# Attention heads into a two-layer network: earlier input loads on other queues, and a later place for the softmax reciprocals

## The chip, the core and the metric

The kernel runs on one core of a Trainium2 chip. The core has five instruction streams: TensorE (PE, matrix products), VectorE (DVE), ScalarE (ACT), GpSimd (POOL) and SyncE (SP). Each works through its own list in order; semaphores tie the lists together. DMA transfers can be issued from SP, ACT and POOL. The metric is the device time in microseconds (us), as the median of several runs.

## What is computed

The reference takes q, k and v of shape (8 images, 12 heads, 448 positions, 64) and two weight matrices, 768 x 2048 and 2048 x 768. All are float32. Cut to what matters:

```python
scores = scale * q @ k.T                 # per image and head, scale = 1/sqrt(64)
attn   = exp(scores - max)               # softmax over the last axis
attn   = attn / (attn.sum(-1) + 1e-9)
x      = attn @ v                        # heads side by side: 3584 tokens x 768
h      = x @ w_in                        # 3584 x 2048
out    = maximum(0.01 * h, h) @ w_out    # 3584 x 768
```

## The kernel before, in words

**Work units.** Two heads of one image make a pair, so an image has 6 pairs and the whole input has 48. The 448 positions are cut into 4 chunks of 112. The order of all instructions is written out by hand; no planner moves them.

**One pair.** `load` brings q, k and v of the pair in as float32, three transfers of 224 KB. `cast` turns them into bfloat16; the v tiles carry a block of ones beside v, so that the product with v also yields the row sums of the exponentials. `transposes` turns q and k on PE and DVE copies the result to SBUF (qkT). `scores` makes one chunk of k against all q for both heads, and `expo` takes the exponential on ACT. `pv` multiplies the exponentials of one head (j = 0 or 1) with v; DVE copies the result to a tile t, and SP sends the row of sums from t to a tile in which the sums lie across partitions (sums). `recips` waits for that, takes the reciprocal on DVE (rec), and SP writes it to DRAM (d) and reads it back twice, broadcast over 64 partitions each (rb). `muls` multiplies t with rb on DVE and writes the slice of xT that belongs to this pair. xT is the input of the network, with tokens along the free axis.

**The network.** `mlp(i)` works on a block of 384 or 512 tokens (`cuts`), alternating, as 448 is no multiple of 128. It makes 16 tiles of h, each from 6 products over xT (line 233), with the leaky ReLU on ACT, and then the output in rows of 128 tokens, each half from 16 products (line 245) with a copy on DVE (line 250) and a store on SP. It is a generator that yields after each product, so it can be spread between other work.

**The order.** A pair step u has eight slots, s0 to s7. In step u the scores of pair u are made (s0 and s4, exponentials in s0, s1, s4, s5), the products with v of pair u-1 (s2 and s6), and the transposes of pair u+1 (s7). Before the change `recips(u-2)` stands in s1 and `muls(u-2)` in s7. POOL loads pair u+6 and, in the first steps, two weight transfers in s0, and casts pair u+2 in s3. The first 8 steps run without the network: that is the head. From then on the products of one block are spread evenly over the 48 slots of six steps, beginning with slot s0. Each block starts just after the last `muls` it needs. The last block runs alone at the end.

**Start.** Before the first step, the identity for the transposes is made on POOL, the ones in the v tiles are set on DVE, and POOL issues the loads of pairs 0 to 5 with the casts of pairs 0 and 1 between them. The weights are cast from float32 to bfloat16 by the transfer itself, in eight pieces of 768 KB (as written), on POOL.

Lines of the profile to know: 94 loads, 106, 107 and 109 casts, 129 weights, 148 and 152 transposes and their copy, 160 scores, 170 exponentials, 176 products with v, 181 their copy to t, 186 sums, 190 reciprocal, 192 d, 195 rb, 208 multiply into xT, 224 stores.

Of the kernel before, what the change touches and what calls it, by code (L numbers as in the profile page):

```python
# [10 lines left out]
BF16 = mybir.dt.bfloat16  # L11
# [6 lines left out]
def kernel(  # L18
# [9 lines left out]
    nc = tc.nc  # L28

    B, H, S, D = q.shape  # L30
    DM, DF = moe_w_in.shape
    P = 128
    HP = H // 2
    SC = 112
    NSC = S // SC
    KD = DM // P
    MD = DF // P
    NW = DM // 2
    NU = B * HP
    scale = 1.0 / float(D) ** 0.5  # L40

    cuts = [((b * S) // P) * P for b in range(B)] + [B * S]
# [3 lines left out]
    const_pool = ctx.enter_context(tc.tile_pool(name="const", bufs=1))  # L46
    w_pool = ctx.enter_context(tc.tile_pool(name="weights", bufs=1))
    ld_pool = ctx.enter_context(tc.tile_pool(name="ld", bufs=6))
    cast_pool = ctx.enter_context(tc.tile_pool(name="cast", bufs=3))
    v_pool = ctx.enter_context(tc.tile_pool(name="vones", bufs=1))  # L50
    qk_pool = ctx.enter_context(tc.tile_pool(name="qk", bufs=3))
    exp_pool = ctx.enter_context(tc.tile_pool(name="exp", bufs=3))
    t_pool = ctx.enter_context(tc.tile_pool(name="pvt", bufs=3))
    r_pool = ctx.enter_context(tc.tile_pool(name="rec", bufs=3))
    xT_pool = ctx.enter_context(tc.tile_pool(name="xT", bufs=3))
    h_pool = ctx.enter_context(tc.tile_pool(name="h", bufs=2))
# [5 lines left out]
    ps_pv = ctx.enter_context(tc.tile_pool(name="ps_pv", bufs=1, space=PSUM))  # L62
    ps_mm = ctx.enter_context(tc.tile_pool(name="ps_mm", bufs=2, space=PSUM))

    ident = const_pool.tile([P, P], BF16)
    make_identity(nc, ident)

    NV = 4  # L70
    v_sb = [v_pool.tile([SC, 2, NSC, 2 * D], BF16, name=f"v{i}") for i in range(NV)]
    for t in v_sb:
        nc.vector.memset(t[:, 0, :, D:], 1.0)
        nc.vector.memset(t[:, 1, :, :D], 1.0)

    w_in_sb = w_pool.tile([P, KD, DF], BF16)
    w_out_sb = w_pool.tile([P, MD, DM], BF16)
# [4 lines left out]
    q_sb = {}  # L82
    k_sb = {}

    def load(u):
        if u >= NU:
            return
        b, hp = divmod(u, HP)  # L90
        raw[u] = []
        for a, name in ((q, "fq"), (k, "fk"), (v, "fv")):
            t = ld_pool.tile([SC, 2, NSC, D], F32, name=name)
            nc.gpsimd.dma_start(  # L94
                out=t.rearrange("p h so d -> p h (so d)"),
                in_=a[b, 2 * hp:2 * hp + 2].rearrange("h (p so) d -> p h (so d)", so=NSC),
            )
            raw[u].append(t)

    def cast(u):  # L100
        if u >= NU:
            return
        fq, fk, fv = raw.pop(u)
        q_sb[u] = cast_pool.tile([SC, NSC, 2, D], BF16, name="q")
        k_sb[u] = cast_pool.tile([SC, NSC, 2, D], BF16, name="k")
        nc.gpsimd.tensor_copy(q_sb[u].rearrange("p so h d -> p h so d"), fq)  # L106
        nc.gpsimd.tensor_copy(k_sb[u].rearrange("p so h d -> p h so d"), fk)  # L107
        for j in range(2):
            nc.gpsimd.tensor_copy(v_sb[u % NV][:, j, :, j * D:(j + 1) * D], fv[:, j])  # L109

    load(0)
    cast(0)
    load(1)
    load(2)
    load(3)
    cast(1)
    for i in range(4, 6):
        load(i)
    w_steps = []
    for i in range(4):  # L120
        w_steps.append((w_in_sb[:, :, ts(i, DF // 4)], w_in_v[:, :, ts(i, DF // 4)]))
# [3 lines left out]
    def load_w(n):  # L125
        for _ in range(n):
            if w_steps:
                o, i = w_steps.pop(0)
                nc.gpsimd.dma_start(out=o, in_=i)


    qk_t = {}
# [5 lines left out]
    def get_xT(i):  # L138
        if xT[i] is None:
            xT[i] = xT_pool.tile([P, KD, 4 * P], BF16, name="xT")  # L140
        return xT[i]

    def transposes(u):
        b, hp = divmod(u, HP)
        tr = ps_tr.tile([P, 2, S], BF16, name="tr")
        for i, src in enumerate((q_sb[u], k_sb[u])):
            for so in range(NSC):
                nc.tensor.transpose(  # L148
                    tr[:, i, ts(so, SC)], src[:, so], ident[:SC, :SC]
                )  # L150
        qk_t[u] = qk_pool.tile([P, 2, S], BF16, name="qkT")
        nc.vector.tensor_copy(qk_t[u], tr)  # L152
# [14 lines left out]
    def expo(u, c):  # L167
        if u not in e_t:
            e_t[u] = exp_pool.tile([SC, 2, NSC, S], BF16, name="e")
        nc.scalar.activation(e_t[u][:, :, c, :], sc_t.pop((u, c))[:, :, :S], AX.Exp, scale=scale)  # L170

    def pv(u, j):
        b, hp = divmod(u, HP)
        ps = ps_pv.tile([P, S], F32, name="pv")
        for c in range(NSC):
            nc.tensor.matmul(  # L176
                ps, v_sb[u % NV][:, j, c, :], e_t[u][:, j, c, :],
                start=(c == 0), stop=(c == NSC - 1),
# [9 lines left out]
    def recips(u):  # L188
        rec = r_pool.tile([SC, 2, NSC], F32, name="rec")
        nc.vector.reciprocal(rec, bc_t[u])  # L190
        d = d_pool.tile([2, S], F32, name="d")
        nc.sync.dma_start(out=d.rearrange("j (p c) -> p j c", c=NSC), in_=rec)
        rb = r_pool.tile([P, S], F32, name="rb")
        for j in range(2):
            nc.sync.dma_start(out=rb[ts(j, D), :], in_=d[j:j + 1, :].to_broadcast([D, S]))  # L195
        bc_t[u] = rb

    def muls(u):
        b, hp = divmod(u, HP)
        lo, hi = b * S, (b + 1) * S  # L200
        for j in range(2):
            pl = slice(j * D, (j + 1) * D)
            for i in (b, b + 1):
                a, z = max(lo, cuts[i]), min(hi, cuts[i + 1] if i < B else hi)
                if a >= z:
                    continue
                x = get_xT(i)
                nc.vector.tensor_mul(  # L208
                    x[pl, hp, a - cuts[i]:z - cuts[i]],
                    pv_s[u, j][pl, a - lo:z - lo],  # L210
                    bc_t[u][pl, a - lo:z - lo],
                )
        del pv_s[u, 0], pv_s[u, 1], bc_t[u], e_t[u], qk_t[u]
# [13 lines left out]
    def mlp(i):  # L227
        n = cuts[i + 1] - cuts[i]
        h = h_pool.tile([P, MD, 4 * P], BF16, name="h")
        for m in range(MD):  # L230
            ps = ps_mm.tile([P, 4 * P], F32, name="mm")
            for kk in range(KD):
                nc.tensor.matmul(  # L233
                    ps[:, :n], w_in_sb[:, kk, ts(m, P)], get_xT(i)[:, kk, :n],
                    start=(kk == 0), stop=(kk == KD - 1),
                )
                if kk == KD - 1:
                    nc.scalar.activation(h[:, m, :n], ps[:, :n], AX.Prelu, alpha=0.01)  # L238
                yield n
        for c in range(n // P):  # L240
            o = o_pool.tile([P, DM], F32, name="o")
            for w in range(2):
                ps = ps_mm.tile([P, 4 * P], F32, name="mm")
                for m in range(MD):
                    nc.tensor.matmul(  # L245
                        ps[:, :NW], h[:, m, ts(c, P)], w_out_sb[:, m, ts(w, NW)],
                        start=(m == 0), stop=(m == MD - 1),
                    )
                    if m == MD - 1:
                        nc.vector.tensor_copy(o[:, ts(w, NW)], ps[:, :NW])  # L250
                    yield NW
            store(o, cuts[i] + c * P)


    def slots(u):

        on = u < NU

        def s0():
            if on:  # L260
                scores(u, 0)
                scores(u, 1)
                expo(u, 0)
            load(u + 6)
            if u < 6:
                load_w(2)

        def s1():
            if on:
                expo(u, 1)  # L270
            if u >= 2:
                recips(u - 2)

        def s2():
            if 1 <= u <= NU:
                pv(u - 1, 0)

        def s3():
            cast(u + 2)

        def s4():
            if on:
                scores(u, 2)
                scores(u, 3)
                expo(u, 2)

        def s5():
            if on:
                expo(u, 3)

        def s6():
            if 1 <= u <= NU:
                pv(u - 1, 1)

        def s7():
            if u + 1 < NU:
                transposes(u + 1)
            if u >= 2:
                muls(u - 2)

        return [s0, s1, s2, s3, s4, s5, s6, s7]

    transposes(0)
    for i in range(B + 1):

        first = 0 if i == 0 else HP * i + 2
        last = HP * (i + 1) + 2 if i < B else first
        work = [s for u in range(first, min(last, NU + 2)) for s in slots(u)]
        atoms = mlp(i - 1) if i > 0 else iter(())
        total = 0 if i == 0 else MD * KD * (cuts[i] - cuts[i - 1]) + (cuts[i] - cuts[i - 1]) // P * MD * DM  # L310
        used = 0
        for n, s in enumerate(work):
            s()
            while used < total * (n + 1) // len(work):
                step = next(atoms, None)
                if step is None:
                    break
                used += step
        for _ in atoms:
            pass  # L320
# [30 lines left out]
```

## Time and profile before

| | us |
|---|---|
| three runs | 555.23, 542.29, 554.82 |
| median of the runs | 554.82 |
| the profiled execution, its own time | 556.75 |
| span of that execution, first to last instruction | 555.0 |
| head, until the network's first products | 0 to 97 |
| seven blocks beside the pair steps | 97 to 507 |
| last block alone | 507 to 555 |

Busy time in these three parts, each line with its length, then busy time (and number of instructions) of PE, PEld (the loading of stationary operands, beside PE), DVE, ACT and POOL, the granted TensorE clock, the mean share of the DMA engines and GB/s:

```profile
0.00:97.00 97.00, 48.50 (x201) 18.92 (x202) 27.08 (x59) 30.36 (x35) 59.90 (x107) 0.77 0.86 189
97.00:507.00 410.00, 386.95 (x2400) 196.87 (x2399) 183.68 (x334) 191.34 (x271) 142.18 (x244) 0.98 0.39 102
507.00:555.00 48.00, 43.09 (x218) 21.85 (x217) 4.46 (x8) 9.56 (x16) 0.00 (x0) 0.93 0.15 42
```

How to read what follows. A group of instructions is named by its line, engine and operation and by the tiles it writes and reads ("xT<-t,rb"). "[4.59 <-DMA rb<-d]" behind an instruction says that its engine stood idle for 4.59 us before it and that the landing of that transfer ended the wait. The chain of waits is followed back from the last instruction, at each step to what released it; its shares say where the span was spent.

### The profile page before, as it was taken

What the parts mean: (1) busy time and instruction counts of PE and PEld (TensorE: products, weight loads), DVE (VectorE), ACT (ScalarE), POOL (GpSimd) and SP (SyncE); (2) the same over time, 40 slices, a digit from 0 to 9 for tenths busy, and PEclk for the clock granted to TensorE, in tenths of its full rate; (3) what the DMA queues carried; (4) which work ended last, traced back from release to release, by engine and by line L of the source; (5) the groups of instructions that cost most, each with busy time, mean ns of one, the idle gap of its engine ahead of it and who ended that gap; (6) DMA issues with size and microseconds to landing.
All of it is one profiled execution on the core that took longest, in us unless ns stands there. A gap on an engine that the chain in (4) does not pass through costs nothing.

```text
span 555.0 us, 7636 instructions
## 1 busy us (share of the span) xinstructions
PE 478.5 (86%) x2816; PEld 237.6 (43%) x2816; DVE 215.2 (39%) x400; ACT 231.3 (42%) x321; POOL 202.1 (36%) x350
## 2 busy tenths in 40 slices
PE   2744447999899999999599999999699999996996
PEld 1211113455444554555244554555244555552453
DVE  2221335444433564444234545464253553341011
ACT  3332223563346334654165335644365246601400
POOL 8963724454532433643225335455141210000000
PEclk9998555999989999999799999999899999997999
DMA  5999944344533354535433436354341222122013
GB/s 147 249 230 242 242 109 103 98 118 120 156 96 83 89 155 123 135 90 154 113 82 94 122 102 172 97 145 115 95 118 30 79 62 50 31 63 60 1 28 87
DMA packets 52774, 62.21 MB, mean 112 GB/s; under 512 B 28672, under 2 KB 39936, under 8 KB 52736
## 3 DMA queue, kind: packets, MB, share of 16 engines
q0 software_dynamic: 16768, 39.33, 27.8%
q1 hardware_dynamic: 35968, 22.38, 16.6%
q8 instruction: 22, 0.36, 0.3%
q14 instruction: 16, 0.13, 0.1%
HBM read 56.62 MB, written 11.18 MB: 122 GB/s over the span
## 4 chain that ended last, share of the span: by engine, by line
PE 65%; DMA 22%; DVE 7%; SPq 2%; issue 2%; POOL 2%; DVEq 0%; POOLq 0%
PE mm L233 25%; PE mm L245 19%; PE pv L176 11%; DMA d<-rec 8%; DMA sums<-t 7%; DMA rb<-d 7%; PE sc L160 6%; DVE xT L208 3%; PE tr L148 3%; DVE qkT L152 2%; SPq L195 1%; DVE o L250 1%; DMA fv<-in_v_dram 1%; SPq L224 1%; POOL fq L94 0%
## 5 line engine op out<-in xcount | busy, mean ns | idle before, releaser
L170 ACT ACTIVATE e<-sc 112x896 bf16<-112x896 f32 x192 | 168.5, 915 | 188.8 <-PE sc L160 188.6
L233 PE MATMUL mm<-xT,w_in_sb 128*128 128x384 bf16 (+1 forms) x768 | 173.0, 364 | 20.9 <-DVE xT L208 19.4
L245 PE MATMUL mm<-w_out_sb,h 128*128 128x384 bf16 x896 | 162.1, 326 | 0.8 <-DVE o L250 0.6
L176 PE MATMUL pv<-e,v 112*128 112x448 bf16 x384 | 100.9, 390 | 29.9 <-DVE t L181 29.9
L109 POOL CAST v<-fv 112x256 bf16<-112x256 f32 x96 | 38.3, 404 | 230.9 <-PE pv L176 230.6
L181 DVE COPY t<-pv 128x448 f32<-128x448 f32 x96 | 59.6, 620 | 149.0 <-PE pv L176 148.7
L233 PEld LDWEIGHTS <-w_in_sb 128*128 128x128 bf16 x768 | 72.0, 100 | 102.7 <-issue 47.7
L238 ACT ACTIVATE h<-mm 128x384 bf16<-128x384 f32 (+1 forms) x128 | 69.9, 546 | 109.2 <-PE mm L233 109.1
L208 DVE TENSOR_TENSOR xT<-t,rb 64x384 bf16<-64x384 f32 (+2 forms) x144 | 87.1, 630 | 68.2 <-DMA rb<-d 67.0
L245 PEld LDWEIGHTS <-h 128*128 128x128 bf16 x896 | 83.6, 98 | 67.0 <-issue 13.7
L176 PEld LDWEIGHTS <-v 112*128 112x128 bf16 x384 | 38.9, 103 | 74.7 <-issue 47.8
L160 PE MATMUL sc<-qkT 64*112 64x448 bf16 x384 | 63.4, 411 | 8.6 <-DVE qkT L152 6.4
L250 DVE COPY o<-mm 128x384 f32<-128x384 f32 x56 | 31.1, 555 | 63.6 <-PE mm L245 63.1
L152 DVE COPY qkT<-tr 128x896 bf16<-128x896 bf16 x48 | 30.0, 624 | 33.5 <-PE tr L148 32.8
L160 PEld LDWEIGHTS <-qkT 64*112 64x112 bf16 x384 | 18.7, 135 | 45.6 <-DVE qkT L152 24.8
L94 POOL DMA_DIRECT2D fv<-in_v_dram x48 | 31.9, 664 | 11.9 <-DMA w_in_sb<-in_moe_w_in_dram 6.5
L106 POOL CAST q<-fq 112x512 bf16<-112x512 f32 x48 | 34.0, 708 | 4.2 <-PE tr L148 1.5
L94 POOL DMA_DIRECT2D fk<-in_k_dram x48 | 31.9, 665 | 7.2 <-DMA w_out_sb<-in_moe_w_out_dram 4.6
L94 POOL DMA_DIRECT2D fq<-in_q_dram x48 | 32.1, 668 | 4.6 <-issue 0.2
L107 POOL CAST k<-fk 112x512 bf16<-112x512 f32 x48 | 31.8, 662 | 0.1
L148 PE MATMUL tr<-ident,q 112*128 112x112 bf16 x192 | 19.3, 228 | 11.2 <-POOL q L106 11.2
L148 PEld LDWEIGHTS <-q 112*128 112x128 bf16 x192 | 15.4, 106 | 21.1 <-POOL q L106 12.4
(14 smaller groups left out, 52.8 us busy)
## 6 DMA issues: line engine op xcount, KB each, us to landing
fq<-in_q_dram POOLq DMA_DIRECT2D x48, 224.0 KB, 3.4
fk<-in_k_dram POOLq DMA_DIRECT2D x48, 224.0 KB, 3.9
fv<-in_v_dram POOLq DMA_DIRECT2D x48, 224.0 KB, 4.2
rb<-d SPq DMA_DIRECT2D x96, 112.0 KB, 3.0
w_in_sb<-in_moe_w_in_dram POOLq DMA_DIRECT2D x4, 768.0 KB, 12.7
w_out_sb<-in_moe_w_out_dram POOLq DMA_DIRECT2D x4, 768.0 KB, 17.7
out_dram<-o SPq DMA_DIRECT2D x8, 336.0 KB, 3.3
out_dram<-o SPq DMA_DIRECT2D x8, 288.0 KB, 2.7
```

The lines of the kernel that those rows point to most:

```text
L94: nc.gpsimd.dma_start(out=t.rearrange("p h so d -> p h (so d)"), in_=a[b, 2 * hp:2 * hp + 2].rearrange("h (p so) d -> p h (so d)", so=NSC),)
L109: nc.gpsimd.tensor_copy(v_sb[u % NV][:, j, :, j * D:(j + 1) * D], fv[:, j])
L148: nc.tensor.transpose(tr[:, i, ts(so, SC)], src[:, so], ident[:SC, :SC])
L152: nc.vector.tensor_copy(qk_t[u], tr)
L160: nc.tensor.matmul(ps[:, j, :S], qk_t[u][j * D:(j + 1) * D, 1, ts(c, SC)], qk_t[u][j * D:(j + 1) * D, 0, :], start=True, stop=True,)
L170: nc.scalar.activation(e_t[u][:, :, c, :], sc_t.pop((u, c))[:, :, :S], AX.Exp, scale=scale)
L176: nc.tensor.matmul(ps, v_sb[u % NV][:, j, c, :], e_t[u][:, j, c, :], start=(c == 0), stop=(c == NSC - 1),)
L181: nc.vector.tensor_copy(t, ps)
L208: nc.vector.tensor_mul(x[pl, hp, a - cuts[i]:z - cuts[i]], pv_s[u, j][pl, a - lo:z - lo], bc_t[u][pl, a - lo:z - lo],)
L233: nc.tensor.matmul(ps[:, :n], w_in_sb[:, kk, ts(m, P)], get_xT(i)[:, kk, :n], start=(kk == 0), stop=(kk == KD - 1),)
L238: nc.scalar.activation(h[:, m, :n], ps[:, :n], AX.Prelu, alpha=0.01)
L245: nc.tensor.matmul(ps[:, :NW], h[:, m, ts(c, P)], w_out_sb[:, m, ts(w, NW)], start=(m == 0), stop=(m == MD - 1),)
```

## The change

The loads of pairs 0 to 5 are issued first of all, before the identity is made: those of pair 0 on SP (q, v) and ACT (k), those of pairs 1 to 5 on SP. Later loads stay on POOL. The ones are set on POOL instead of DVE. Pair 0 is cast by three engines (q DVE, k ACT, v POOL), pairs 1 and 2 by POOL before the first step. In the steps, `load` moves from s0 to s3, and `cast` from pair u+2 in s3 to pair u+3 in s5. Of the weights, four pieces go out in step 0 and two each in steps 4 and 5, instead of two in each of the first four steps.

`recips(u-2)` moves from s1 to s3, behind the first `pv` of the step; `muls` moves from s7 of step u = pair + 2 to s2 of step u = pair + 3, ahead of that `pv`. A block of the network begins at slot s3 instead of s0, three slots later, so that the same `muls` still stands in the slot before it; there is one pair step more at the end. The pools for cast q and k and for t have 4 buffers instead of 3, and there are 5 v tiles instead of 4.

```diff
-    cast_pool = ctx.enter_context(tc.tile_pool(name="cast", bufs=3))
+    cast_pool = ctx.enter_context(tc.tile_pool(name="cast", bufs=4))
...
-    t_pool = ctx.enter_context(tc.tile_pool(name="pvt", bufs=3))
+    t_pool = ctx.enter_context(tc.tile_pool(name="pvt", bufs=4))
...
-    ident = const_pool.tile([P, P], BF16)
-    make_identity(nc, ident)
-    NV = 4
+    NV = 5
     v_sb = [v_pool.tile([SC, 2, NSC, 2 * D], BF16, name=f"v{i}") for i in range(NV)]
-    for t in v_sb:
-        nc.vector.memset(t[:, 0, :, D:], 1.0)
-        nc.vector.memset(t[:, 1, :, :D], 1.0)
...
-    def load(u):
+    def load(u, queues=(nc.gpsimd,) * 3):
...
-            nc.gpsimd.dma_start(
+            eng.dma_start(
...
-    def cast(u):
+    def cast(u, by=(nc.gpsimd.tensor_copy,) * 3):
...
-    load(0)
-    cast(0)
-    load(1)
-    load(2)
-    load(3)
-    cast(1)
-    for i in range(4, 6):
-        load(i)
...
+    load(0, (nc.sync, nc.scalar, nc.sync))
+    for i in range(1, 6):
+        load(i, (nc.sync,) * 3)
+    ident = const_pool.tile([P, P], BF16)
+    make_identity(nc, ident)
+    for t in v_sb:
+        nc.gpsimd.memset(t[:, 0, :, D:], 1.0)
+        nc.gpsimd.memset(t[:, 1, :, :D], 1.0)
+    cast(0, (nc.vector.tensor_copy, nc.scalar.copy, nc.gpsimd.tensor_copy))
+    cast(1)
+    cast(2)
...
         def s0():
...
-            load(u + 6)
-            if u < 6:
-                load_w(2)
 
         def s1():
             if on:
                 expo(u, 1)
-            if u >= 2:
-                recips(u - 2)
 
         def s2():
+            if u >= 3:
+                muls(u - 3)
             if 1 <= u <= NU:
                 pv(u - 1, 0)
 
         def s3():
-            cast(u + 2)
+            if 2 <= u <= NU + 1:
+                recips(u - 2)
+            load(u + 6)
+            if u == 0:
+                load_w(4)
+            elif u in (4, 5):
+                load_w(2)
...
         def s5():
             if on:
                 expo(u, 3)
+            cast(u + 3)
...
         def s7():
             if u + 1 < NU:
                 transposes(u + 1)
-            if u >= 2:
-                muls(u - 2)
...
+    steps = [s for u in range(NU + 3) for s in slots(u)]
+    begin = [8 * (HP * (i + 1) + 2) + 3 for i in range(B)]
...
-    for i in range(B + 1):
-        first = 0 if i == 0 else HP * i + 2
-        last = HP * (i + 1) + 2 if i < B else first
-        work = [s for u in range(first, min(last, NU + 2)) for s in slots(u)]
-        atoms = mlp(i - 1) if i > 0 else iter(())
+    for s in steps[:begin[0]]:
+        s()
+    for i in range(B):
+        work = steps[begin[i]:begin[i + 1]] if i + 1 < B else []
+        atoms = mlp(i)
```

More of the change, by code (lines that the diff above doesn't have):

```diff
@@ L91, in load @@
         raw[u] = []
-        for a, name in ((q, "fq"), (k, "fk"), (v, "fv")):
+        for a, name, eng in zip((q, k, v), ("fq", "fk", "fv"), queues):
             t = ld_pool.tile([SC, 2, NSC, D], F32, name=name)
-            nc.gpsimd.dma_start(
+            eng.dma_start(
                 out=t.rearrange("p h so d -> p h (so d)"),
@@ L105, in cast @@
         k_sb[u] = cast_pool.tile([SC, NSC, 2, D], BF16, name="k")
-        nc.gpsimd.tensor_copy(q_sb[u].rearrange("p so h d -> p h so d"), fq)
-        nc.gpsimd.tensor_copy(k_sb[u].rearrange("p so h d -> p h so d"), fk)
+        by[0](q_sb[u].rearrange("p so h d -> p h so d"), fq)
+        by[1](k_sb[u].rearrange("p so h d -> p h so d"), fk)
         for j in range(2):
-            nc.gpsimd.tensor_copy(v_sb[u % NV][:, j, :, j * D:(j + 1) * D], fv[:, j])
-    load(0)
-    cast(0)
-    load(1)
-    load(2)
-    load(3)
-    cast(1)
-    for i in range(4, 6):
-        load(i)
+            by[2](v_sb[u % NV][:, j, :, j * D:(j + 1) * D], fv[:, j])
     w_steps = []
@@ L297, in s7 @@
                 transposes(u + 1)
-            if u >= 2:
-                muls(u - 2)
         return [s0, s1, s2, s3, s4, s5, s6, s7]
+    steps = [s for u in range(NU + 3) for s in slots(u)]
+    begin = [8 * (HP * (i + 1) + 2) + 3 for i in range(B)]
+    assert begin[B - 1] == 8 * (NU + 2) + 3
     transposes(0)
-    for i in range(B + 1):
-        first = 0 if i == 0 else HP * i + 2
-        last = HP * (i + 1) + 2 if i < B else first
-        work = [s for u in range(first, min(last, NU + 2)) for s in slots(u)]
-        atoms = mlp(i - 1) if i > 0 else iter(())
-        total = 0 if i == 0 else MD * KD * (cuts[i] - cuts[i - 1]) + (cuts[i] - cuts[i - 1]) // P * MD * DM
+    for s in steps[:begin[0]]:
+        s()
+    for i in range(B):
+        work = steps[begin[i]:begin[i + 1]] if i + 1 < B else []
+        n = cuts[i + 1] - cuts[i]
+        total = MD * KD * n + n // P * MD * DM
         used = 0
-        for n, s in enumerate(work):
+        atoms = mlp(i)
+        for j, s in enumerate(work):
             s()
-            while used < total * (n + 1) // len(work):
+            while used < total * (j + 1) // len(work):
                 step = next(atoms, None)
```

## The prediction

> Prediction: **538 us**, faster, by some 17 us. Working follows.
>
> **What bounds the kernel now.** I read the page's busy times and chain first, then the stages, then the chain in order of time, then the waits at the edges between images.
>
> ```profile
> PE 478.5 (86%) x2816; PEld 237.6 (43%) x2816; DVE 215.2 (39%) x400; ACT 231.3 (42%) x321; POOL 202.1 (36%) x350
> PE 65%; DMA 22%; DVE 7%; SPq 2%; issue 2%; POOL 2%; DVEq 0%; POOLq 0%
> ```
>
> TensorE carries most of the chain, yet 22% of it is DMA, and by line nearly all of that is the small transfers of the softmax sums (d 8%, sums 7%, rb 7%). The stages (columns: length, then busy of PE, PEld, DVE, ACT, POOL, granted clock, DMA share, GB/s) show where:
>
> ```profile
> 14.00:28.00 14.00, 10.14 (x44) 3.42 (x42) 3.06 (x6) 5.18 (x6) 14.00 (x24) 1.00 1.07 247
> 28.00:50.00 22.00, 12.34 (x52) 4.70 (x49) 4.85 (x11) 8.63 (x10) 13.12 (x23) 1.00 1.21 231
> 50.00:70.00 20.00, 5.92 (x24) 2.31 (x24) 4.58 (x8) 3.45 (x4) 10.76 (x19) 0.54 1.13 244
> ...
> 216.00:274.00 58.00, 51.24 (x336) 26.98 (x336) 23.96 (x43) 27.86 (x40) 25.13 (x42) 0.97 0.46 118
> ```
>
> From 14 to 70 us the DMA engines are full and PE is idle more than half the time; from 97 us PE is nearly full. In the head the chain is a ring:
>
> ```profile
> 40.95 7.98 DMA d<-rec
> 49.53 7.00 DMA rb<-d
> 56.62 1.96 DVE xT L208 x2
> 58.84 6.31 DMA d<-rec
> ```
>
> One pair's reciprocal goes out (d), comes back broadcast (rb), is multiplied, and only then does DVE reach the next pair's reciprocal. The reciprocals start at 27.3, 40.7, 58.6, 73.8, 83.4 and 90.8 us: 13.4, 17.9 and 15.2 us apart while the weights load, then 9.5 and 7.4. An unhindered step takes 6.6 us (first scores at 25.01 and 31.61). Later the same ring shows as a wait at an image's edge, here on DVE:
>
> ```profile
> 265.43 0.62 DVE L152 COPY qkT<-tr 128x896 bf16<-128x896 bf16 x1 [0.42 <-PE tr L148]
> 270.65 0.62 DVE L208 TENSOR_TENSOR xT<-t,rb 64x448 bf16<-64x448 f32 x1 [4.59 <-DMA rb<-d]
> 273.04 0.62 DVE L208 TENSOR_TENSOR xT<-t,rb 64x448 bf16<-64x448 f32 x1 [1.77 <-DMA rb<-d]
> ```
>
> DVE waits 6.4 us for rb, and PE, which needs this last slice of xT, stands 5.83 us. Waits of PE on xT or on the o copies behind it at the edges: 2.5, 1.2, 5.8, 1.2, 4.6, 0.4 and 5.2 us (the last with 0.6 just ahead of it), 20.8 us together.
>
> **What the skill says.** The Trainium skill, "DMA: Bandwidth & Descriptors", section "Issuing engines are not separate DMA queues": transfers from sync, scalar and gpsimd share 16 engines and interleave; another issuer saves issue time only. The trace agrees: d on SP's queue lands in 2.5 us (median) but takes 8.0 while POOL's weights run. "TensorE: Matmul & The Clock Gate", Part 1: the array starts at half clock and needs sustained work. Here four pv matmuls take 1.65 us in the head, 0.76 later. The same page, "Architectural detail", calls VectorE strict FIFO; the ring above is that. "GPSIMD Engine Reference", section 4.1: one-input operations are about line rate there, the basis for the moved memsets.
>
> **The change, part by part.**
>
> *First loads.* 18 transfers of 224 KB leave POOL (18 x 0.66 = 12 us of its time) and go to SP (17) and ACT (1), ahead of everything. SP then issues for about 17 x 0.55 = 9.4 us (0.55 from the rb issues), and no sums transfer is due before 14 us. ACT's one issue and k cast, about 0.6 each, stand ahead of its first exponential (8.3 us before) and delay nothing; they and DVE's q cast (0.6, taken from POOL's 0.65) run side by side where POOL did them in turn. Ten memsets on POOL, bounds 0.2 (ident's) to 0.4 (a v cast of that size), taken as 0.3: 3 us, hidden under the first landing (about 3.4 us) and under step 0, which hides the casts of pairs 1 and 2 too. First scores: 7.6 becomes 6.4 us. Pair 1's transposes, which waited 3.1 us for POOL, follow the last scores of step 0 (6.4 + 3.1 = 9.5 us), so step 1 starts at 11.3 us, not 15.6, and step 2 at 17.9, not 25.0. The first reciprocal needs sums issued at about 17.1; with the 5.8 us that this took under load, it starts at 23, not 27.3.
>
> *Weights.* All eight remain on POOL; four now go out in one step, four in steps 4 and 5, the later loads behind them. The bytes before the weights are in are the same. DMA share times length up to 70 us: 7.7 + 15.0 + 26.6 + 22.6 = 71.9. At the full stages' mean of 1.15 from 2 us on (before, the first 14 us ran at 0.55) this ends at 64.5 us. w_out is first read half an image after the first matmul of L233, near 120 us. POOL waits behind the weights for up to 4 us now; pair 7's data, behind four w_in, is due at about 40 us for use past 50. I cost this at nothing; without that cover PE would wait for casts.
>
> *The later reciprocal and multiply.* On DVE the order was multiply(k), reciprocal(k+1), t copy(k+2,0); now it is multiply(k), t copy, reciprocal. So the ring keeps d, rb and the multiply and gains one t copy, 0.62 us. SP's queue changes alike: one sums transfer moves ahead of d; the other still queues behind rb, and the output stores behind all of them, as before. What does change is the distance in slots from the second t copy of a pair to its multiply: 9 become 12; to the reciprocal 3 become 5. An image's matmuls start 3 slots later too, so the multiply still stands just before them. A slot is 8.5/8 = 1.06 us in images of 384 tokens, 10.1/8 = 1.26 in those of 512. The deeper pools (cast, t, v) only make this legal; I cost them at nothing.
>
> *Head.* Reciprocal 0 at 23, rounds of 15.5 us until 64.5 (2.7 of them), the other 2.3 at 8.5 + 0.6, then 7.7 to the last multiply's end: 64.5 + 20.9 + 7.7 = 93.1, against 98.5. **-5 us.** Bounds: rounds that stay long to the end, +16; rounds of 9 us throughout (23 + 45.5 + 7.7 = 76), -22.
>
> *Edges.* Three slots absorb up to 3.2 us of each wait on xT: 2.3 + 0.8 + 3.2 + 0.8 + 3.2 + 3.2 = 13.5. Off goes 1.5: rb is now issued close to POOL's next loads (the second half's v cast releases them in slot 6), and where that happened before, at 256.1 us, the second rb took 4.2 us instead of 3.0. **-12 us.** Bounds 0 and -20.8.
>
> The last image's own 48 us of matmuls after 507 us stay. Sum: -17 of the span of 555.0, so 538; with 1.75 us around it the profiled execution, 556.75, would give 539.7. The median of the three runs, 554.82, is 1.9 below that execution: 538.
>
> **Rivals.**
> 1. *The head comes free.* If the small transfers no longer suffer from the weights (fewer in flight once the first loads have left their queue), rounds take about 9 us: -22 in the head, -14 at the edges: 519. Against it: as many weights, the same engines.
> 2. *The ring still paces everything.* Rounds with output stores already take 9.3 to 10.1 us against a step of 8.5 (reciprocals at 133.7, 143.0, 153.1). 0.6 more and rb beside the loads use up the new slots. Head -3, edges -2: 550.
> 3. *The weights press longer (slower).* w_out, put off to steps 4 and 5, keeps the DMA full through rounds 3 to 5 and the last multiply. Then 23 + 5 x 15.5 + 14 = 114.5, +16 on 98.5, and with nothing won at the edges 571. It decides if w_out's last part lands after 95 us; I expect 65 to 70. POOL running ahead of PE speaks against it.
> 4. *It doesn't do what it says:* the "two steps later" is two slots; on DVE only a swap. That is built into the main case.
>
> **Chances.** Main case 0.52 (own range 528 to 550), rival 1 0.20, rival 2 0.19, rival 3 0.09. About 2% is what a measurement here can tell, so faster means under 543.7. Main case 0.78 of its chance, all of rival 1, a tenth of rival 2: 0.63. Slower: rival 3, 0.09. Same: 0.28. The three runs spread over 542 to 555, so the state of one run alone can carry a case over the bound. Range 518 to 553: it takes in rival 1's value and rival 2's, and leaves out rival 3 and the best of rival 1.
>
> **What would show it.** First scores near 6.4 us and step 2 near 18; first reciprocal near 23; the first full L233 group near 93; DMA share above 1 from about 3 us and ending near 65; PE waits on xT of at most 2.6 us an edge; few waits of a reciprocal for sums (19.2 us before). The forecast is wrong if rounds in the head are 9 us or 15 throughout, if t copies late by rb stop PE inside an image, or if PE waits for casts.

## The result and the profile after

The changed kernel is slower. Its median is 561.8 us (4 runs, 560.0 to 562.8) against 551.2 us for the kernel before on the same chip (4 runs, 542.3 to 555.2); the ratio is 1.031, with a 95% interval of 1.021 to 1.041. The ratio is taken over each kernel's runs within 1.5% of its fastest, so without the two runs of about 555 us of the kernel before, near which its profiled execution (556.75 us) lies; by the medians it is 1.019, and why that kernel's runs differ so much is open. On another chip the unaltered changed kernel gave 1.013 [1.006, 1.021] (`a1_changed_again`, below). The forecast was 538 us, 0.97 of the median before.

The changed kernel's profiled execution took 560.0 us, its span 558.2. The page's busy times and chain by engine and line:

```profile
PE 476.3 (85%) x2816; PEld 237.8 (43%) x2816; DVE 194.6 (35%) x393; ACT 231.8 (42%) x322; POOL 187.0 (33%) x340
...
DMA 47%; PE 33%; DVE 11%; SPq 4%; issue 3%; ACT 0%; DVEq 0%
DMA rb<-d 26%; DMA d<-rec 16%; PE mm L231 14%; PE mm L243 11%; PE pv L174 5%; DMA sums<-t 4%; DVE xT L206 4%; DVE t L179 3%; PE sc L158 3%; SPq L193 2%; PE tr L146 1%; DVE o L248 1%; DVE rec L188 1%; SPq L184 1%; SPq L222 1%
```

TensorE has the same work, but DMA's share of the chain went from 22% to 47%: rb from 7% to 26%, d from 8% to 16%. The ring of the head now runs through most of the kernel. The stages cut at the start and the end of the blocks (length, busy PE, PEld, DVE, ACT, POOL, clock, DMA share, GB/s):

```profile
0.00:98.00 98.00, 47.88 (x209) 18.98 (x210) 23.99 (x54) 31.94 (x37) 53.02 (x103) 0.62 0.89 191
98.00:511.00 413.00, 386.40 (x2389) 197.19 (x2389) 166.07 (x333) 190.32 (x270) 133.96 (x237) 0.98 0.40 100
511.00:558.20 47.20, 41.98 (x218) 21.60 (x217) 4.54 (x9) 9.51 (x16) 0.00 (x0) 0.93 0.15 42
```

The head ends at 98 us, as before. The seven blocks take 413 us, where they took 408.4 (98.0 to 506.4). Nothing came from the head, and the middle lost. The two profiles differ by 3.2 us of span (555.0 and 558.2), so they account for that much of the loss and not for all of it. The clock column of the heads can't be compared: the view of the kernel before gives 1.00 from 14 to 28 us, yet four products with v took 1.68 us at 25.93 there, like those at 149.22 in the changed kernel (1.65 us), where 0.50 was granted. The waits of the whole span, in total, times and longest, say where:

```profile
DVE xT L206 <- DMA rb<-d: 188.8, 66, 11.5
...
PE pv L174 <- DVE t L179: 53.4, 19, 10.2
...
PE mm L231 <- DVE xT L206: 4.9, 3, 2.2
...
DVE rec L188 <- DMA sums<-t: 3.6, 2, 3.2
```

Two waits were cured as forecast: PE on xT 19.4 to 4.9 us, the reciprocal on sums 19.2 to 3.6. What came in their place is larger: VectorE's wait for rb rose from 67.0 to 188.8 us, and PE's wait for the t copy, the next thing on VectorE behind that multiply, from 29.9 to 53.4 us. All of the 29.9 us and 34.7 of the 53.4 lie in the head. For the blocks alone (98 to 511 us after, 98 to 506.4 before), the largest wait of PE is this one after the change, and this one before it:

```profile
PE pv L174 <- DVE t L179: 18.7, 14, 2.5
...
PE mm L233 <- DVE xT L208: 19.4, 7, 5.8
```

In the kernel before, no block had a wait for t. So the edges gave back 14.5 us (19.4 to 4.9), and new waits inside the images took 18.7. The median time of an rb from issue to landing rose from 3.0 to 4.4 us. One step of a 384-token block, in order of time (DVE, SP and POOL alone):

```profile
108.83 0.62 DVE L179 COPY t<-pv 128x448 f32<-128x448 f32 x1
109.48 0.53 SPq L184 DMA_DIRECT2D sums<-t  x1
109.48 0.20 DVE L188 RECIPROCAL rec<-sums 112x8 f32<-112x8 f32 x1
110.11 0.53 SPq L190 DMA_DIRECT2D d<-rec  x1
...
110.49 0.40 POOL L103 CAST v<-fv 112x256 bf16<-112x256 f32 x1 [3.73 <-PE pv L174]
111.02 0.66 POOL L88 DMA_DIRECT2D fq<-in_q_dram  x1
...
111.80 1.12 SPq L193 DMA_DIRECT2D rb<-d  x2
...
116.61 0.62 DVE L206 TENSOR_TENSOR xT<-t,rb 64x448 bf16<-64x448 f32 x1 [4.48 <-DMA rb<-d]
117.47 0.62 DVE L206 TENSOR_TENSOR xT<-t,rb 64x448 bf16<-64x448 f32 x1 [0.24 <-DMA rb<-d]
118.12 0.62 DVE L179 COPY t<-pv 128x448 f32<-128x448 f32 x1
118.77 0.20 DVE L188 RECIPROCAL rec<-sums 112x8 f32<-112x8 f32 x1
```

The round takes 9.29 us (109.48 to 118.77) where TensorE needs 8.5. The t copy lets PE make the second product with v; that lets POOL cast v and, behind the cast, issue the next loads at 111.02, just ahead of rb at 111.80. So 672 KB are under way or due when rb starts, it lands late, the multiply is late, and so is the next t copy. In the kernel before the same stretch of VectorE and SP reads:

```profile
108.46 0.20 DVE L190 RECIPROCAL rec<-sums 112x8 f32<-112x8 f32 x1 [1.16 <-DMA sums<-t]
...
108.69 0.31 SPq L192 DMA_DIRECT2D d<-rec  x1
...
111.17 1.11 SPq L195 DMA_DIRECT2D rb<-d  x2
...
113.21 0.66 POOL L94 DMA_DIRECT2D fq<-in_q_dram  x1
...
114.25 1.56 DVE L208 TENSOR_TENSOR xT<-t,rb 64x448 bf16<-64x448 f32 x2
...
116.84 0.20 DVE L190 RECIPROCAL rec<-sums 112x8 f32<-112x8 f32 x1 [1.04 <-DMA sums<-t]
```

Here rb goes out 2 us ahead of the loads. From the reciprocal to the end of the multiplies 7.35 us pass (108.46 to 115.81), and VectorE then waits another 1.04 us for the next sums: the ring has room in the step. Of the 33 steps from 90 us on that still have loads, rb went out within 2.5 us behind POOL's first load in 2 before, and in 26 after.

### The profile page after: what moved, and what is told of

The parts are those of the page before. It is cut to its first block, busy times and chain, and to the rows that moved or that the text cites. A ratio compares the mean times of both kernels' runs of the same rounds, so it can differ in the third digit from the quotient of the medians.

```text
span 558.2 us, 7565 instructions
## 1 busy us (share of the span) xinstructions
PE 476.3 (85%) x2816; PEld 237.8 (43%) x2816; DVE 194.6 (35%) x393; ACT 231.8 (42%) x322; POOL 187.0 (33%) x340
## 3 DMA queue, kind: packets, MB, share of 16 engines
q1 hardware_dynamic: 40048, 26.28, 19.4%
## 4 chain that ended last, share of the span: by engine, by line
DMA 47%; PE 33%; DVE 11%; SPq 4%; issue 3%; ACT 0%; DVEq 0%
DMA rb<-d 26%; DMA d<-rec 16%; PE mm L231 14%; PE mm L243 11%; PE pv L174 5%; DMA sums<-t 4%; DVE xT L206 4%; DVE t L179 3%; PE sc L158 3%; SPq L193 2%; PE tr L146 1%; DVE o L248 1%; DVE rec L188 1%; SPq L184 1%; SPq L222 1%
## 5 line engine op out<-in xcount | busy, mean ns | idle before, releaser
L231 PE MATMUL mm<-xT,w_in_sb 128*128 128x384 bf16 (+1 forms) x768 | 170.2, 360 | 7.0 <-DVE xT L206 4.9
L243 PE MATMUL mm<-w_out_sb,h 128*128 128x384 bf16 x896 | 164.3, 328 | 0.0
L174 PE MATMUL pv<-e,v 112*128 112x448 bf16 x384 | 99.9, 387 | 53.4 <-DVE t L179 53.4
L206 DVE TENSOR_TENSOR xT<-t,rb 64x384 bf16<-64x384 f32 (+2 forms) x144 | 66.4, 487 | 189.4 <-DMA rb<-d 188.8
L231 PEld LDWEIGHTS <-w_in_sb 128*128 128x128 bf16 x768 | 71.5, 99 | 85.2 <-issue 28.4
L150 DVE COPY qkT<-tr 128x896 bf16<-128x896 bf16 x48 | 29.9, 622 | 20.8 <-PE tr L146 20.1
L88 POOL DMA_DIRECT2D fk<-in_k_dram x42 | 27.9, 665 | 6.8 <-DMA w_in_sb<-in_moe_w_in_dram 5.0
L100 POOL CAST q<-fq 112x512 bf16<-112x512 f32 x47 | 29.4, 625 | 2.4 <-POOL v L103 1.5
L88 POOL DMA_DIRECT2D fq<-in_q_dram x42 | 28.1, 669 | 6.1 <-DMA w_in_sb<-in_moe_w_in_dram 1.3
L101 POOL CAST k<-fk 112x512 bf16<-112x512 f32 x47 | 29.6, 630 | 0.5 <-DMA fk<-in_k_dram 0.5
L88 POOL DMA_DIRECT2D fv<-in_v_dram x42 | 27.9, 664 | 5.5 <-DMA w_in_sb<-in_moe_w_in_dram 3.1
L146 PEld LDWEIGHTS <-q 112*128 112x128 bf16 x192 | 15.6, 107 | 14.5 <-DVE q L100 4.8
## 6 DMA issues: line engine op xcount, KB each, us to landing
w_in_sb<-in_moe_w_in_dram POOLq DMA_DIRECT2D x4, 768.0 KB, 15.5
```

Of the source, the lines that this page charges most:

```text
L88: eng.dma_start(out=t.rearrange("p h so d -> p h (so d)"), in_=a[b, 2 * hp:2 * hp + 2].rearrange("h (p so) d -> p h (so d)", so=NSC),)
L146: nc.tensor.transpose(tr[:, i, ts(so, SC)], src[:, so], ident[:SC, :SC])
L174: nc.tensor.matmul(ps, v_sb[u % NV][:, j, c, :], e_t[u][:, j, c, :], start=(c == 0), stop=(c == NSC - 1),)
L206: nc.vector.tensor_mul(x[pl, hp, a - cuts[i]:z - cuts[i]], pv_s[u, j][pl, a - lo:z - lo], bc_t[u][pl, a - lo:z - lo],)
L231: nc.tensor.matmul(ps[:, :n], w_in_sb[:, kk, ts(m, P)], get_xT(i)[:, kk, :n], start=(kk == 0), stop=(kk == KD - 1),)
L243: nc.tensor.matmul(ps[:, :NW], h[:, m, ts(c, P)], w_out_sb[:, m, ts(w, NW)], start=(m == 0), stop=(m == MD - 1),)
```

## The experiments

Four theories stood. R: the ring d, rb, multiply, t copy, reciprocal paces the steps. S: of that, the added t copy (0.62 us) is the cost. L: the moved loads and weights cost the time. C, formed after the first four runs: the loads released just ahead of rb are the cost. Kernels that are compared with each other ran on one chip, beside runs of the kernel before; ratios are to those.

### One order turned round, one undone, and the two halves alone

`e1_ring_cut`, on the changed kernel, so that no multiply stands between two reciprocals:

```diff
         def s2():
-            if u >= 3:
-                muls(u - 3)
             if 1 <= u <= NU:
                 pv(u - 1, 0)
         def s3():
             if 2 <= u <= NU + 1:
                 recips(u - 2)
+            if u >= 3:
+                muls(u - 3)
...
-    begin = [8 * (HP * (i + 1) + 2) + 3 for i in range(B)]
+    begin = [8 * (HP * (i + 1) + 2) + 4 for i in range(B)]
```

> The changed kernel with one order turned round on VectorE: in s3 first recips(u-2), then muls(u-3) (blocks begin one slot later), so that no multiply stands between two reciprocals. Theory R (the ring d, rb, multiply, t copy, reciprocal paces each pair step, 9.6 us where TensorE needs 8.5): steps in blocks of 384 tokens go back to 8.5 us, rb waits of VectorE fall from 189 us to under 40, the median falls to 530 to 542. Theory L (the moved loads and weights cost the time): stays at 556 to 562. Theory S (only the added 0.62 us of the t copy in the ring): falls too, so this run does not tell S from R.

`e2_recip_first`, on the changed kernel:

```diff
         def s2():
             if u >= 3:
                 muls(u - 3)
+            if 2 <= u <= NU + 1:
+                recips(u - 2)
             if 1 <= u <= NU:
                 pv(u - 1, 0)
         def s3():
-            if 2 <= u <= NU + 1:
-                recips(u - 2)
```

> The changed kernel with the reciprocal ahead of the t copy again (s2: muls(u-3), recips(u-2), pv(u-1,0)): the ring loses its 0.62 us, everything else stays. Theory S: steps of 384-token blocks fall from 9.6 to 9.0 us, 24 or so of them, and the head's rounds too: 542 to 548. Theory R with rb beside the loads: the ring stays, rb still lands in 4 to 5 us, 552 to 558. Theory L: 560.

`e3_loads_alone` is the changed kernel with the old slots:

```diff
         def s1():
             if on:
                 expo(u, 1)
+            if 2 <= u <= NU + 1:
+                recips(u - 2)
         def s2():
-            if u >= 3:
-                muls(u - 3)
...
         def s7():
...
+            if 2 <= u <= NU + 1:
+                muls(u - 2)
...
-    begin = [8 * (HP * (i + 1) + 2) + 3 for i in range(B)]
+    begin = [8 * (HP * (i + 1) + 2) for i in range(B)]
```

> The changed kernel with recips in s1 and muls in s7 of step pair+2 and the blocks' begin as in the kernel before: the loads, weights and casts part alone. Theory R: the seven blocks run as in the kernel before, head 3 to 5 us shorter: 545 to 552. Theory L: 558 to 562.

`e4_moves_alone` is the reverse: the kernel before, with the four lines of `recips` and `muls`, `begin` and the t pool of the changed one.

> The kernel before with only the later recips and muls (and the begin of the blocks, the extra step and 4 t buffers): loads, weights, casts as before. Theory R: 558 to 566, with rb landing in over 4 us. Theory L: 540 to 550.

| kernel | median us | ratio to before (560.8), 95% | DVE waits for rb, us | rb, issue to landing, us |
|---|---|---|---|---|
| e1_ring_cut | 534.8 | 0.952 [0.947, 0.957] | 2.7 | 3.1 |
| e2_recip_first | 542.2 | 0.966 [0.961, 0.971] | 96.6 | 3.1 |
| e3_loads_alone | 555.2 | 0.989 [0.983, 0.996] | 70.2 | 2.9 |
| e4_moves_alone | 573.0 | 1.018 [1.010, 1.027] | 220.1 | 4.6 |

L falls: the loads alone gain 1%, and the moves alone lose 2%, with the same long rb as the whole change. R holds so far: without the ring VectorE hardly waits for rb. On this chip, where the kernel before took 560.8 us and not 551.2, e3 and e4 came out 3 and 7 us above R's ranges. e2 was meant to take 0.62 us from the ring and took far more; S, which forecast 542 to 548, has its time right. But rb's own landing time went back to 3.1 us, which a shorter ring alone doesn't explain. Its timeline shows the order turned: after the reciprocal at 104.20 rb went out at 105.95, the first load at 106.46. That gave theory C. In e1, too, rb mostly stood ahead of the loads (it was behind in 5 of 32 steps), so e1 alone doesn't tell the ring from the order of the transfers.

### Where the loads stand against rb

`a1_changed_again` is the changed kernel itself, to compare with on this chip.

> The changed kernel itself, unaltered, on the chip of the three runs beside it, so that they can be compared with it directly. Both theories: about 3% above the kernel before of the same chip.

`e5_loads_elsewhere`, on the changed kernel. POOL issues the next loads behind the first v cast, which the first product with v releases; VectorE's and SP's orders are left alone:

```diff
         for j in range(2):
             by[2](v_sb[u % NV][:, j, :, j * D:(j + 1) * D], fv[:, j])
+            if j == 0 and then is not None:
+                load(then)
...
-            load(u + 6)
+            if u == 0:
+                load(6)
...
-            cast(u + 3)
+            cast(u + 3, then=u + 7)
```

> The changed kernel with POOL issuing the next pair's loads between the two v casts (released by the first product with v of a step) and no longer behind the second one. VectorE's and SP's orders stay. Theory C (the loads, released just ahead of rb, make rb late: the order of the two transfers decides): rb lands in about 3 us, waits for rb fall from 189 us to 100 to 130, and the time by 10 to 18 us. Theory T (the t copy's 0.62 us and the sums transfer ahead of d in the ring decide): within 4 us of the changed kernel.

`e7_d_before_sums`, on the changed kernel, where `pv(u - 1, 0)` leaves its sums transfer to s3:

```diff
             if 1 <= u <= NU:
-                pv(u - 1, 0)
+                pv(u - 1, 0, send=False)
...
                 recips(u - 2)
+            if 1 <= u <= NU:
+                send_sums(u - 1, 0)
```

> The changed kernel with SP sending d and rb ahead of the first sums transfer of the step, as before the change; VectorE's order (t copy ahead of the reciprocal) stays. rb is then issued 0.4 to 0.5 us sooner after the reciprocal, still 0.3 us behind the first load. Theory T with SP's share: 4 to 8 us less than the changed kernel, the ring about 0.4 us shorter. Theory C: little, under 5 us less, unless rb slips ahead of the loads; then 10 or more.

The kernel before took 561.0 us here. The changed one took 567.1 (1.013 [1.006, 1.021]), less of a loss than the 3% expected. e5 took 535.9 (0.957 [0.952, 0.963]), 31 us less than the changed kernel; e7 548.2 (0.975 [0.966, 0.984]), 19 less, with runs from 542 to 551. Of these e5 alone tells C from T, the theory that the t copy and the sums transfer are the cost: both still stand in its ring, and the time fell by about twice what C had asked for. Its timeline:

```profile
107.34 0.66 POOL L88 DMA_DIRECT2D fk<-in_k_dram  x1
...
108.39 0.20 DVE L190 RECIPROCAL rec<-sums 112x8 f32<-112x8 f32 x1
109.02 0.53 SPq L192 DMA_DIRECT2D d<-rec  x1
...
111.95 1.12 SPq L195 DMA_DIRECT2D rb<-d  x2
...
115.18 1.27 DVE L208 TENSOR_TENSOR xT<-t,rb 64x448 bf16<-64x448 f32 x2 [3.40 <-DMA rb<-d]
115.19 0.66 POOL L88 DMA_DIRECT2D fq<-in_q_dram  x1
```

The next loads now go out at 115.19, when rb has landed, and those of the step before (107.34) meet d instead, which takes 2.9 us in place of 1.7. rb lands in a median of 3.0 us. The round shown is 8.75 us (108.39 to 117.14), and VectorE's 163 us of waits for rb, more than I expected (100 to 130), are mostly covered. PE's wait for t is 39.8 us, after 60.7 in the changed kernel beside it; in the heads, up to 98 us in both, it is 36.0 and 36.1, so the gain lies in the blocks, where 24.6 us (98 to 518.1) became 3.8 (98 to 490.1).

In e7, 0.40 us less between reciprocal and d (0.23, not 0.63) was enough for rb to slip ahead in about half of the steps: in its step at 114.77 rb goes out at 116.75, the first load at 118.65. Over the 32 or 33 steps with loads, rb stood behind them in 26 of the changed kernel, 28 of a1 and 30 of e4, which lost against the kernel before; in 17 of e7; and in 2 to 5 of the kernel before, e1, e2 and e3, and none of e5.

In the changed kernel the order changes seldom: rb is behind in 19 steps running, then not for 7, then behind again in 7. I read this as two orders that each keep themselves up: with rb ahead, as in e7's step at 114.77 (8.49 us to the next reciprocal), the round fits into PE's 8.5 us, PE sets the pace and the loads come later still; with the loads ahead, the round is longer than 8.5 us, the t copy sets the pace, and the loads follow it at once. That they keep themselves up is argued from the timelines; no run tests it alone. C fits every run so far, and the timeline shows R as the way by which a late rb reaches PE. No run cuts the ring and leaves rb behind the loads, so what a late rb costs without the ring is not shown.

`e11_before_elsewhere` puts the same edit into the kernel before (`cast(u + 2, then=u + 7)`).

> The kernel before with the next pair's loads between its two v casts, nothing else. Theory C: the late rb at the edges of its 384-token blocks (4.2 to 6.6 us from issue to landing where it met the loads) was the same meeting, so its edge waits of 21 us fall by half and the time by 8 to 15 us. Rival (the kernel before only lacks slots at the edges): within 5 us of the kernel before.

It missed: 558.9 us, ratio 1.004 [1.001, 1.006]. In that kernel's order the new place is the bad one. rb went out within 2.5 us behind a first load in 14 of 33 steps, where the kernel before had 2 of 33, and its median landing rose from 3.0 to 3.7 us. So the run says nothing on the edge waits without such meetings; that stays untried. No place of the loads is good in itself, only one against the ring's phase.

### The head

With the ring cut, e1's rounds while the weights load were still 12.4, 17.2 and 15.3 us, and its chain there ran over d, SP's issue of rb, sums, and d again: SP waits for d ahead of rb, and the sums transfer stands behind.

`e8_two_rings_cut` moves d and rb behind the second sums transfer (`spread`, the DMA half of `recips`) and the multiply to s5:

```diff
             if on:
                 expo(u, 3)
+            if u >= 3:
+                muls(u - 3)
             cast(u + 3)
...
                 pv(u - 1, 1)
+            if 2 <= u <= NU + 1:
+                spread(u - 2)
...
-    begin = [8 * (HP * (i + 1) + 2) + 3 for i in range(B)]
+    begin = [8 * (HP * (i + 1) + 2) + 6 for i in range(B)]
```

> On top of the cut ring (reciprocal in s3, multiply behind it, now in s5; blocks begin 6 slots into the step): SP sends d and rb only after the second sums transfer of the step (s6), so that no sums transfer waits behind a landing of d of the same step. Theory: the head, which in the run with the cut ring still went round over d and sums in 12.4, 17.2 and 15.3 us, gets rounds of about 10, and the network starts near 80 us instead of 92: 522 to 530, about 7% below the kernel before. Rival (the head is bound by the bytes of loads and weights themselves): as with the cut ring, 533 to 537.

It missed: 550.6 us (0.980 [0.970, 0.989], runs from 545 to 562), rounds of 15.0, 16.3 and 15.3 us, the network at 94 us. Its chain in the head shows why:

```profile
38.33 6.05 DMA d<-rec
...
44.40 6.18 DMA rb<-d
...
50.67 1.16 DVE xT L210 x2
51.85 0.99 DVE xT L210 x2
52.87 0.62 DVE t L179
...
54.10 7.84 DMA d<-rec
```

I had made a new ring: d now waits on SP for the second sums transfer, that for the t copy, that for the multiply, and that for rb. Both d and rb are in it.

`e9_cut_and_elsewhere` is e1 with e5's edit. `e10_rb_last` is e9 with only rb moved behind the second sums transfer; d stays in s3:

```diff
         nc.sync.dma_start(out=d.rearrange("j (p c) -> p j c", c=NSC), in_=rec)
+        bc_t[u] = d
+
+    def spread(u):
+        d = bc_t[u]
         rb = r_pool.tile([P, S], F32, name="rb")
...
                 pv(u - 1, 1)
+            if 2 <= u <= NU + 1:
+                spread(u - 2)
```

> The cut ring (t copy, reciprocal, multiply in s3) together with the next pair's loads between the two v casts. Theory C says that the two edits cure the same wait: with the ring cut, VectorE waited only 2.7 us for rb in all, so moving the loads as well adds little: 528 to 535, at most 1% under the cut ring alone. Rival (loads also cost elsewhere, at sums or at stores): 520 to 527.

> As the run beside it, and SP sends rb only behind the second sums transfer of the step (s6), so that SP no longer stands waiting for d ahead of that transfer; d stays in s3. Theory (the head goes round over d and sums because SP waits for d): rounds of 10 to 11 us in place of 12 to 17 while the weights load, the network starts before 82 us, 515 to 525. Rival (bytes bind the head): rounds and start as in the run beside it. As two ways of changing SP's order have moved a ring before, a new one over rb, multiply, second t copy and sums is possible: 6 to 10 us a step, at or under the 8.5 us of TensorE outside the head.

The kernel before took 556.9 us here. e9 took 529.6 (0.951 [0.947, 0.955], e1 had 0.952): with the ring cut, the place of the loads is worth nothing that can be told from none. e10 took 513.8, a ratio of 0.923 [0.918, 0.927], and beats both kernels. Its rounds were 6.1, 14.9, 9.0, 12.2, 9.1; the forecast of 10 to 11 holds for their mean (10.3) and not for each. The network starts at 84.6 us, later than the 82 expected. Of the 15.2 us between the spans of e9 and e10 (527.0 and 511.8), 6.0 lie ahead of the network's first product (90.6 and 84.6) and 9.2 behind it, which the theory of the head had not named and whose cause is open. The chain on its page:

```profile
PE 79%; DMA 13%; DVE 5%; issue 1%; SPq 0%; ACT 0%; DVEq 0%
```

It is TensorE's for 79% of the span, and the blocks take 380.7 us (85.0 to 465.7), PE busy for 377.1 of them.

## Why the prediction was wrong

By stage, the sum for a span of 538 us had the head end at 93.1 and left 396.9 for the blocks and 48 for the end; measured were 98.0, 413.0 and 47.2. So 5 us of the miss are the head's, and 16 the blocks'.

- **Start and first loads: right.** First scores at 6.57 us (forecast 6.4), step 2 at 17.5 (17.9), first reciprocal at 22.8 (23). DMA share fell under 1 near 66 us (64.5). Two readings were off. PE was busy for 28.4 of the 56 us from 14 to 70, so idle about half of the time and not more. And the 0.76 us of four products with v is the chain's figure; the timeline, from which the 1.65 comes, has 0.92 (at 107.71).
- **Head, -5 us: wrong size.** The full group of L231 starts at 98.1 us, not 93.1. The term at fault is the rounds. Three long ones (13.2, 16.9 and 16.8) carried the ring to 69.7 us, where the sum had 2.7 of 15.5 up to 64.5, as a round begun under load ends under it. Then came 9.5 and 9.6, and 9.3 to the end of the last multiply, where it had 2.3 of 9.1, and 7.7.
- **Edges, the slots: right.** PE's waits on xT fell to 4.9 us, and no edge waited over 2.2 (forecast at most 2.6).
- **Edges, -12 us: the step that failed.** It said "Off goes 1.5", a single price for rb beside POOL's loads, taken from one rb that had left just ahead of them. The next rb of that trace, at the very edge that the prediction shows, had left behind them, and VectorE waited 4.59 and 1.77 us for its two halves:

```profile
264.94 0.66 POOL L94 DMA_DIRECT2D fq<-in_q_dram  x1
...
265.85 1.12 SPq L195 DMA_DIRECT2D rb<-d  x2
```

After the change rb left behind them in 26 of 33 steps. The sum treated the ring as latency to be hidden in slots; it is a round that must fit into the 8.5 us step. I had priced its growth at the t copy's 0.62 us. Beside it stand 0.40 us on SP (reciprocal to d 0.63, not 0.23: "SP's queue changes alike" got no price) and 1.4 us in rb's median landing. The round became 9.29 us in the step shown, and the waits came back inside the images as PE's wait for t: 18.7 us in the blocks, where it had been none, against 14.5 won at the edges. "t copies late by rb stop PE inside an image" stood among the prediction's own signs of being wrong.

- **Rival 2 was the right mechanism**, down to "rb beside the loads use up the new slots". Its size, 550 us, was too small: I let a lag stop at zero gain, though a round that outlasts the step costs in every step.
- **Rivals 1 and 3** did not happen: the rounds stayed long while the weights loaded, and the last weights landed at 67.4 us.
- **"On DVE only a swap" was true and misjudged.** The swap of reciprocal and t copy turned the order of two DMA transfers; undoing that swap alone gave 0.966 of the kernel before.

That a program crosses from one order of rb and loads to the other is shown by e2, e5 and e7.

## What to carry to other kernels

When a chain of small transfers passes twice through an in-order engine, add up its round and hold it against the step; spare slots hide a latency, not a round longer than the step. Turn the order on the engine so that no instruction that waits for the last transfer stands between two that start the first, and follow the issuing queue in the same way: of two such orders here one, e10, gained 3% over the cut ring's 0.951, and the other, e8, fell 3% behind it (0.980). Ask of each bulk transfer which event releases it, and whether that event is part of the ring: if so, it can meet the small transfers in most steps and not now and then, as it did here in 26 of 33.

## What the runs showed of the hardware

- A 112 KB rb read of the changed kernel, from 90 us on, took 4.9 us in the median (up to 6.9) when it left within 2.5 us behind the first of three loads of 224 KB, 3.2 when it left ahead of them, and 2.8 with no load near. The Trainium skill, "DMA: Bandwidth & Descriptors", section "Queues, rings and completion order", has each DMA engine go round its queues packet by packet; the head agrees: an rb issued at 29.02 us landed at 34.6, while a weight transfer issued at 16.1 landed only at 36.9, so rb was delayed and not held until it was done. In the blocks no rb landed before a load that had left ahead of it, so they don't tell.
- VectorE's multiply of two SBUF tiles stretches while POOL casts. In e7 a multiply of 64x448 that elsewhere takes 0.62 us took 1.95, from 111.82, as POOL cast from 112.11 to 113.29. The Trainium skill, "SBUF — State Buffer", section "Who interferes with whom", says that such an instruction contends with GpSimd's reads. Before the change this multiply averaged 0.63 us over its forms, and 70 of 144 overlapped a cast; after it the average was 0.49, and 25 overlapped one. VectorE's time in it fell from 87.1 to 66.4 us, which did not show in the kernel's time.
- Long waits at the edges went with a lower clock of TensorE. In the kernel before, 0.50 was granted from 270.2 to 277.0 us, beside the wait of 5.83, and from 505.7 to 512.5, beside one of 4.57; from 215 to 222, with a wait of 0.79, it was 1.00. In e5, with no wait of such length in the blocks, it was 1.00 from 100.1 to 480. Three products of 512 columns took 1.60 us at 273.71, and eight took 1.90 at 279.14. So such an edge cost TensorE more than its wait, which the prediction's sum left out.
